# Mirroring most of batch 0 and storing the empty rows of the buckets in two parts

## The chip, the cores and the metric

One core of one Trainium2 chip. The metric is device time in microseconds (us), from one launch. The kernel is a float32 attention over eight batches, followed by a mixture of experts (MoE) that takes the attention's rows.

## The reference

```
# u, v: 8 x 1856 x 256   z: 8 x 1856 x 64   (S = 1856)
scores = (z @ z.transpose(0, 2, 1)) / S
x = u * (maximum(scores, 0) ** 2 @ v)          # then 14848 rows of 256
g = argmax(x @ w_group); e = argmax(x @ w_expert[g])      # 4 groups of 4 experts
h = maximum(x @ w1[g, e], 0)                              # 256 -> 1024
out = softmax weight of g * softmax weight of e * (h @ w2[g, e])
```

The scores of a batch are a symmetric matrix, since both factors are z. Both halves carry the same numbers.

## The kernel before, in words

**Attention.** A batch's 1856 queries are cut into four chunks c = 0 to 3, its 1856 keys into 15 tiles of 128 (the last has 64). One step s is one key tile of one chunk; 60 steps make a batch, s = 0 to 59 is batch 0. For a step, TensorE forms the scores in two matmuls (`sc`), ScalarE (ACT) takes relu and the square (`r`), VectorE (DVE) splits the square into a rounded part `ah` and a rest `al` (a cast and a subtraction), and TensorE multiplies these with the values in six matmuls (`o`: `ah` by `vl`, `ah` by `vh`, `al` by `vh`, for two halves of the output). Scores of a step are made some steps ahead of its `o` matmuls. At the end of a chunk DVE multiplies `o` with u (`xT`), splits it (`xl`), and four matmuls (`pl`) give the routing logits.

**Mirror.** In batches 1 to 7 a block of scores below the diagonal is not computed. When the block above it has been made, DVE transposes it in 32 by 32 pieces (`mt`), SyncE's (SP's) queue stores it to DRAM (`sym`), and four loads bring it back turned (`at`). A step that takes its tile from `at` has no `sc` matmuls, no relu and no square: ACT makes one cast (`ah`) and DVE one subtraction (`al`). Batch 0 computes all its blocks. Batches 1 to 7 have chunks of 512, 512, 512 and 320 queries, batch 0 of 512, 512, 416 and 416.

**Routing.** Each token's row of 1056 bytes (256 values and a few words) is scattered by POOL into the bucket of its expert in DRAM (`bucket`, 16 buckets of `CAPB` rows). A bucket is read to a fixed capacity of 832 to 1216 rows, so rows behind the last token must be empty: `prefill` stores them from a constant tile `padrow`. There are 32 such stores of 640 rows (660 KB) on SP's queue, put in steps 1 to 41 of batch 0 by the list `PFILL`.

**Experts.** The buckets are sorted by their counts; the register values `eli` and `rli` hold, for the j-th, the expert and the first row. The first four (NOLD) are worked on in ten smaller blocks 0 to 9, the others as wider ones. Per block: SP loads the block's rows transposed (`xp`) and a little `meta`; DVE copies (`xf`), ACT casts (`xh_m`), DVE subtracts (`xl_m`); TensorE makes `ph`, ACT and DVE split it (`hh`, `hl`), TensorE makes `yT`; the result goes through a transposing DMA (`yr`) and is scattered to the output. SP's queue also loads the weights of an expert (`raw_e2`, `raw_e3`, four pieces of 512 KB each), two blocks and more ahead. SP, like each engine, carries out its instructions in the order in which they stand.

Of the kernel before, what the change touches and what calls it, by code (L numbers as in the profile page):

```python
# [19 lines left out]
P = 128  # L20
# [9 lines left out]
def tile_glu_attn_moe(  # L30
# [22 lines left out]
    NQ = 4  # L53
    MB = (1, B)
    EDGE = [512, 512, 416, 416], [0, 512, 1024, 1440]
    INNER = [512, 512, 512, S - 1536], [0, 512, 1024, 1536]
    QW, QO = ([(INNER if MB[0] <= b < MB[1] else EDGE)[i] for b in range(B)] for i in range(2))
    ZW = [512, 512, 512, S - 1536]
# [3 lines left out]
    RU = 2 * RW  # L62
    CAPB = (N + 511) // 512 * 512 + 512
    CMAX = (max(caps) + P - 1) // P * P
# [15 lines left out]
    NOLD = 4  # L80
    PFILL = [1 + i for i in range(17)] + [18 + 5 * i // 3 for i in range(2 * NE - 17)]
    assert CMAX % (2 * P) == 0
    FRZ = min(512, min(caps[:NEARLY]))
    assert min(caps[:NEARLY]) > FRZ or len(set(caps)) == 1

# [8 lines left out]
    def cst(name, shape, dt=F32):  # L94
        return pool.tile(shape, dt, tag=name, bufs=1, name=name)
# [25 lines left out]
    def bank(pl, tag, name):  # L121
        return pl.tile([P, 512], F32, tag=tag, name=name)

    bucket = tc.dram_tile([NROW + OVT, RW], I32, name="bucket")
    views = dram_disjoint_views(bucket, B * NQ * NT)

# [177 lines left out]
    def mirrored(b, c, k):  # L304
        return MB[0] <= b < MB[1] and KB[c] < MC and k // KT < MC and POS[k // KT] < c

# [30 lines left out]
    def key(b, c, i):  # L337
        if (b, c) == (B - 1, NQ - 1):
            return (0, 1, 12, 2, 3, 14, 4, 5, 13, 6, 7, 8, 9, 10, 11)[i]
        return KORD[c][i] if MB[0] <= b < MB[1] else i  # L340

    NS = len(steps)
    hl = {}
    oacc = {}
    ut = {}

    def scores(s):
# [27 lines left out]
        ah = new_z(f"ah_{s}")[:, 0:w]  # L375
        mirror = MB[0] <= b < MB[1] and KB[c] < MC and k // KT < MC and c < POS[k // KT]
        if i in ((ACT_TWICE if b + 1 < B else ACT_LAST)[c] if MB[0] <= b < MB[1] else ()) and s >= NK:
            held(nc.scalar.activation(out=ah, in_=a, func=AF.Square))
            held(nc.scalar.activation(out=a, in_=a, func=AF.Square))  # L379
        else:  # L380
            held(nc.scalar.activation(out=a, in_=a, func=AF.Square))  # L381
            held(nc.vector.tensor_copy(out=ah, in_=a))  # L382
# [3 lines left out]
        else:  # L386
            al = None
            nc.vector.tensor_sub(out=ah[TAIL:P, :], in0=a[TAIL:P, :], in1=f32(ah[TAIL:P, :]))
        if mirror:
            put_mirror(b, c, k, a)  # L390
        hl[s] = (ah, al)

# [27 lines left out]
    def chunk_end(s):  # L420
# [85 lines left out]
        defer(s + LG + (1 if XO else 0), logits_out)  # L506
        wait = 5 if last else 12 if b == 0 and c < 2 else (17 if c == 1 and b < B - 1 else 15) if s + 1 < NS - NK else 8
        alone = b == B - 1 and c >= NQ - 2
# [148 lines left out]
    def sort_experts(final=False):  # L657
# [289 lines left out]
    def next_view():  # L947
        ocnt[0] += 1
        return oviews[ocnt[0] - 1]

    def prefill(i):
        r0, n = i // 2 * CAPB + i % 2 * (CMAX // 2), CMAX // 2
        ins = nc.sync.dma_start(
# [47 lines left out]
    for s in range(NS):  # L1001
# [9 lines left out]
        if s == 8:  # L1011
            make_router()
        for i in range(2 * NE):
            if PFILL[i] == s:
                prefill(i)
# [588 lines left out]
```

## Time and profile before

| | |
|---|---|
| median of 3 runs (lowest to highest) | 1425.19 us (1424.57 to 1425.32) |
| the profiled execution | 1423.95 us |
| its span, first to last instruction | 1422.1 us |
| granted clock of TensorE | 1.000 |
| TensorE matmul / weight load busy | 1411.9 us (99%) / 1223.8 us (86%) |
| VectorE / ScalarE / GpSimd busy | 1216.5 us (86%) / 1051.3 us (74%) / 439.0 us (31%) |
| moved by DMA | 256.47 MB |

The profiled execution's own time holds 1.85 us around its span. A sum of edits is made against 1423.95 us, which lies 1.24 us below the median. In the views a start is in us from the span's start; an engine's row has its start, its length, the engine, the line, and output and input by the program's names.

### The profile page before, as it was taken

The numbers are of one execution on the slowest core, as the hardware profiler recorded it, in microseconds if no ns is written. First come the engines' busy times: TensorE is split into PE (matmuls) and PEld (weight loads), VectorE is DVE, ScalarE is ACT, GpSimd is POOL, SyncE is SP. The second block draws the span as 40 slices with busy tenths as digits, with TensorE's granted clock in tenths as the row PEclk, the third lists the DMA queues.
The fourth block names the chain that finished last, engine by engine and source line by source line (L and its number), as shares of the span: only waits on it lengthen the run. The fifth ranks groups of instructions, "written<-read, shape, count | busy, mean of one in ns | idle before, by whom it ended". The sixth has DMA issues, their size and how long they took to land.

```text
span 1422.1 us, 22589 instructions
## 1 busy us (share of the span) xinstructions
PE 1411.9 (99%) x7010; PEld 1223.8 (86%) x7010; DVE 1216.5 (86%) x2436; ACT 1051.3 (74%) x1849; POOL 439.0 (31%) x462
## 2 busy tenths in 40 slices
PE   9999999999999999999999999999999999999998
PEld 7898888888888888888878898988888888899997
DVE  7889999899998999998988667789777888888884
ACT  8887887787887878878776354357777777777773
POOL 0002022220222012202222331332445555555554
PEclk9999999999999999999999999999999999999999
DMA  9997979979899698895987564534555444555552
GB/s 318 328 260 210 235 187 254 230 192 239 195 262 238 160 264 207 223 244 151 243 197 165 116 142 113 122 82 130 126 136 132 126 123 113 138 137 136 139 140 60
DMA packets 400043, 256.47 MB, mean 180 GB/s; under 512 B 244131, under 2 KB 355262, under 8 KB 399920
## 3 DMA queue, kind: packets, MB, share of 16 engines
q1 hardware_dynamic: 387984, 223.97, 63.1%
q0 software_dynamic: 11856, 30.90, 7.7%
q8 instruction: 56, 0.92, 0.3%
q14 instruction: 67, 0.55, 0.1%
q10 hardware_dynamic: 80, 0.13, 0.0%
HBM read 108.29 MB, written 89.21 MB: 139 GB/s over the span
## 4 chain that ended last, share of the span: by engine, by line
PE 92%; DVE 2%; DMA 2%; issue 2%; POOL 1%; ACT 1%; SPq 0%; POOLq 0%; DVEq 0%; ACTq 0%
PE o L408 38%; PE duo_p L887 15%; PE yT L887 6%; PE duo_y L1333 6%; PE sc L370 5%; PE sc L371 5%; PE ph L802 2%; PE ph L803 2%; PE ph L804 2%; PE duo_w L1333 2%; PE duo_x L1333 2%; PE duo_p L1333 2%; PE duo_z L1333 2%; PE pl L483 1%; PE pl L484 1%
## 5 line engine op out<-in xcount | busy, mean ns | idle before, releaser
L408 PE MATMUL o<-ah,vl 128*128 128x512 f32 (+2 forms) x960 | 354.6, 370 | 0.4 <-DVE ah L382 0.4
L408 PE MATMUL o<-ah,vh 128*128 128x512 f32 (+2 forms) x960 | 354.2, 369 | 0.0
L408 PE MATMUL o<-al,vh 128*128 128x512 f32 (+2 forms) x896 | 328.7, 369 | 0.9 <-DVE al L360 0.9
L646 POOL DMA_INDIRECT bucket<-rows,di x121 | 138.6, 1145 | 383.3 <-issue 216.7
L374 ACT ACTIVATE r<-sc 128x512 f32<-128x512 f32 (+2 forms) x312 | 178.8, 573 | 74.4 <-PE sc L371 72.8
L408 PEld LDWEIGHTS o<-ah,vl 128*128 128x128 f32 x960 | 180.2, 188 | 31.0 <-DVE ah L382 1.2
L408 PEld LDWEIGHTS o<-ah,vh 128*128 128x128 f32 x960 | 180.2, 188 | 28.9
L385 DVE TENSOR_TENSOR al<-r,ah 128x512 fp32r<-128x512 f32 (+2 forms) x280 | 187.7, 671 | 19.1 <-ACT r L379 2.2
L930 POOL DMA_INDIRECT out_dram<-y_w,meta_w x92 | 139.3, 1514 | 191.4 <-ACT y_w L924 145.8
L408 PEld LDWEIGHTS o<-al,vh 128*128 128x128 f32 x896 | 167.8, 188 | 27.5 <-DVE al L360 1.2
L887 PE MATMUL duo_p<-hh_w,duo_w 128*128 128x496 f32 (+10 forms) x692 | 178.0, 371 | 0.0
L381 ACT ACTIVATE r<-r 128x512 f32<-128x512 f32 (+2 forms) x280 | 171.4, 612 | 8.9
L887 PEld LDWEIGHTS duo_p<-hh_w,duo_w 128*128 128x128 f32 x692 | 128.6, 188 | 16.7
L382 DVE CAST ah<-r 128x512 fp32r<-128x512 f32 (+2 forms) x280 | 115.9, 414 | 18.8 <-ACT r L381 13.4
L370 PE MATMUL sc<-zm,z2h 128*128 128x512 f32 (+2 forms) x312 | 120.0, 385 | 0.2 <-DVE zm L251 0.2
L371 PE MATMUL sc<-zm,z2l 128*128 128x512 f32 (+2 forms) x312 | 118.9, 381 | 0.0
L310 DVE STREAM_TRANSPOSE mt<-r 128x512 f32<-128x512 f32 x147 | 103.6, 705 | 0.6
L887 PE MATMUL duo_p<-hl_w,duo_w 128*128 128x496 f32 (+10 forms) x346 | 104.1, 371 | 0.0
L360 DVE TENSOR_TENSOR al<-at,ah 128x512 fp32r<-128x512 f32 (+1 forms) x168 | 95.3, 579 | 2.5 <-ACT ah L359 2.3
L359 ACT CAST ah<-at 128x512 fp32r<-128x512 f32 (+1 forms) x168 | 86.1, 531 | 8.8 <-DMA at<-sym 3.9
L807 ACT ACTIVATE hh<-ph 128x512 fp32r<-128x512 f32 (+6 forms) x96 | 45.7, 488 | 39.4 <-PE ph L804 38.6
L887 PE MATMUL yT<-hh,w_e 128*128 128x512 f32 (+6 forms) x352 | 74.1, 328 | 0.0
(259 smaller groups left out, 2874.5 us busy)
## 6 DMA issues: line engine op xcount, KB each, us to landing
sym<-mt SPq DMA_DIRECT2D x126, 256.0 KB
duo_r<-in_w_dram SPq DMA_DIRECT2D x48, 512.0 KB
at<-sym SPq DMA_DIRECT2D x84, 256.0 KB
bucket<-padrow SPq DMA_DIRECT2D x32, 660.0 KB
at<-sym SPq DMA_DIRECT2D x84, 160.0 KB
vr<-in_v_dram SPq DMA_DIRECT2D x23, 512.0 KB
ut<-in_uT_dram SPq DMA_DIRECT2D x23, 512.0 KB
raw_e<-in_w_dram SPq DMA_DIRECT2D x16, 512.0 KB
```

Of the source, the lines that this page charges most:

```text
L310: nc.vector.transpose(out=t2.rearrange("p (j t x) -> p t j x", t=KT, x=32), in_=a.rearrange("p (t j x) -> p t j x", t=KT, x=32))
L370: held(nc.tensor.matmul(ps[:, 0:w], z2h[:, ks], zm, start=True, stop=False))
L371: held(nc.tensor.matmul(ps[:, 0:w], z2l[:, ks], zm, start=False, stop=True))
L374: held(nc.scalar.activation(out=a, in_=ps[:, 0:w], func=AF.Relu, scale=1.0 / S))
L381: held(nc.scalar.activation(out=a, in_=a, func=AF.Square))
L382: held(nc.vector.tensor_copy(out=ah, in_=a))
L385: held(nc.vector.tensor_sub(out=al, in0=a, in1=f32(ah)))
L408: held(nc.tensor.matmul(oa[d][:, 0:QW[b][c]], (vh if q else vl)[:, d0:d0 + P], al if q == 2 else ah, start=(i == 0 and q == 0), stop=end a ...
L646: nc.gpsimd.indirect_dma_start(out=views[(b * NQ + 2 * half + hs[h]) * NT + i], out_offset=bass.IndirectOffsetOnAxis(ap=di[0:n, i0 + i:i0 ...
L887: nc.tensor.matmul(o, wt["2"][f // 2][:, w0:w0 + P], hs[f][q // 2][:, c0:c0 + n], start=(at == 0), stop=(at == 3 * NF - 1))
L930: nc.gpsimd.indirect_dma_start(out=outs(), out_offset=bass.IndirectOffsetOnAxis(ap=meta[0:m, t, 1:2], axis=0), in_=y[0:m], in_offset=None, ...
L1333: nc.tensor.matmul(out, a, b, start=(q == 0 and m in (1, 5)), stop=(q == 2), skip_group_check=True)
```

## The change

Batch 0 gets the chunks of the other batches. All its blocks below the diagonal are taken from the mirror, but those of chunks 0-1 and 0-2: chunk 2 takes 4 tiles (block 1-2), chunk 3 takes 12 (blocks 0-3, 1-3, 2-3). Three of the transposes of chunk 0 are put off by up to six steps (`held_back`). `prefill` stores only the first 512 rows of a bucket, in 16 stores. The rows behind these are stored later, by `fill(j)`, at a row that is taken from the final counts: five small DVE operations behind the final sort make the start rows `sti` (the greater of the count's end and 512), SP loads each start as a register value and stores 768 rows (first four buckets) or 512 rows from there. They stand in the loop over blocks, behind the loads of blocks 1, 2, 3, 5 and 7 (`FILL`). A read of a bucket waits for the fills ahead of it, and a fill for the reads ahead of it. `CAPB` grows by 256 rows.

```
-    MB = (1, B)
-    EDGE = [512, 512, 416, 416], [0, 512, 1024, 1440]
     INNER = [512, 512, 512, S - 1536], [0, 512, 1024, 1536]
-    QW, QO = ([(INNER if MB[0] <= b < MB[1] else EDGE)[i] for b in range(B)] for i in range(2))
+    QW, QO = ([INNER[i] for b in range(B)] for i in range(2))
...
-    CAPB = (N + 511) // 512 * 512 + 512
+    CAPB = (N + 511) // 512 * 512 + 768
...
-    PFILL = [1 + i for i in range(17)] + [18 + 5 * i // 3 for i in range(2 * NE - 17)]
+    PFILL = [1 + 2 * i for i in range(NE)]
...
     def mirrored(b, c, k):
-        return MB[0] <= b < MB[1] and KB[c] < MC and k // KT < MC and POS[k // KT] < c
+        return k // KT < c and (b > 0 or c == NQ - 1 or k // KT > 0)
...
-        return KORD[c][i] if MB[0] <= b < MB[1] else i
+        return KORD[c][i] if b or c else i
...
-        mirror = MB[0] <= b < MB[1] and KB[c] < MC and k // KT < MC and c < POS[k // KT]
-        if i in ((ACT_TWICE if b + 1 < B else ACT_LAST)[c] if MB[0] <= b < MB[1] else ()) and s >= NK:
+        mirror = k // KT > c and (b > 0 or c > 0 or k // KT == NQ - 1)
+        if i in ((ACT_TWICE if b + 1 < B else ACT_LAST)[c]) and s >= NK:
...
-        if mirror:
+        if mirror and s >= NK:
             put_mirror(b, c, k, a)
+        elif mirror:
+            held_back.append((s + (2, 4, 6)[i - NK + 3], lambda: put_mirror(b, c, k, a)))
+        while held_back and held_back[0][0] <= s:
+            held_back.pop(0)[1]()
...
+        if final:
+            st = cst("sst", [P, NE])
+            nc.vector.scalar_tensor_tensor(out=st, in0=ebase, scalar=512.0, in1=base, op0=ALU.add, op1=ALU.max)
...
+            nc.vector.tensor_copy(out=sti, in_=sf)
...
+    def fill(j):
+        regs(j)
+        n = 512 if j >= NOLD else 768
+        at = nc.sync.value_load(sti[0:1, j:j + 1], min_val=512, max_val=(NE - 1) * CAPB + N)
+        nc.sync.dma_start(
+            views[B * NQ * NT + j][ds(at, n), :].rearrange("(p t) w -> p t w", p=P),
+            padrow.unsqueeze(1).to_broadcast([P, n // P, RW]),
+        )
+
     def prefill(i):
-        r0, n = i // 2 * CAPB + i % 2 * (CMAX // 2), CMAX // 2
+        r0, n = i * CAPB, 512
...
-        for i in range(2 * NE):
+        for i in range(NE):
             if PFILL[i] == s:
                 prefill(i)
...
+    FILL = {1: (0, 1), 2: (2, 3), 3: (4, 5, 6, 7), 5: (8, 9, 10, 11), 7: (12, 13, 14, 15)}
...
         more_rows(i)
+        for j in FILL.get(i, ()):
+            fill(j)
```

Where the instructions stand now, first on DVE at the end of batch 0, from the end of chunk 2 (`xT_0_2`) to the split z of batch 1 (`zm_1_0`), which the first scores of batch 1 read. Before:

```order
L430 TENSOR_TENSOR xT_0_2_1130<-o_0_2_0_858,ut_0_2_613 128x416
L430 TENSOR_TENSOR xT_0_2_1130<-o_0_2_1_859,ut_0_2_613 128x416
...
L382 CAST ah_52_1175<-r_52_1173 128x416
L385 TENSOR_TENSOR al_52_1178<-r_52_1173,ah_52_1175 128x416
...
L441 TENSOR_TENSOR xl_0_2_1187<-xT_0_2_1130,xh_0_2_1186 128x416 x2
...
L255 TENSOR_TENSOR z2l_1_0_1249<-zr_1_0_927,z2h_1_0_1248 128x512
...
L271 CAST zm_1_0_1269<-z2h_1_0_1248 64x512
L272 CAST zm_1_0_1269<-z2l_1_0_1249 64x512
```

And of the changed kernel:

```order
L435 TENSOR_TENSOR xT_0_2_1118<-o_0_2_0_896,ut_0_2_628 128x512
L435 TENSOR_TENSOR xT_0_2_1118<-o_0_2_1_897,ut_0_2_628 128x512
L361 TENSOR_TENSOR al_51_1129<-at_0_1_3_1012,ah_51_1128 128x320
L361 TENSOR_TENSOR al_52_1143<-at_0_1_3_1012,ah_52_1142 128x320
L553 COPY lgf_0_0_0_1156<-lgx_0_0_562 128x8x2x40
L558 TENSOR_TENSOR tm_0_0_0_1158<-lgf_0_0_0_1156 128x160
L294 TENSOR_TENSOR vl_1_3_1161<-vr_1_3_960,vh_1_3_1160 128x768
L361 TENSOR_TENSOR al_53_1165<-at_0_1_3_1012,ah_53_1164 128x320
L446 TENSOR_TENSOR xl_0_2_1153<-xT_0_2_1118,xh_0_2_1152 128x512 x2
...
L255 TENSOR_TENSOR z2l_1_0_1209<-zr_1_0_962,z2h_1_0_1208 128x512
...
L271 CAST zm_1_0_1230<-z2h_1_0_1208 64x512
L272 CAST zm_1_0_1230<-z2l_1_0_1209 64x512
```

The subtractions now read the loaded mirror, and the routing of batch 0 (`lgf`, `tm`) has moved behind the end of chunk 2.

Second, on SP, from the load of block 2's rows (`xp_2`) on. Before:

```order
L767 DMA_TRANSPOSE xp_2_10207<-bucket_69 128x4x384
...
L767 DMA_TRANSPOSE xp_3_10387<-bucket_69 128x4x320
...
L767 DMA_TRANSPOSE xp_4_10566<-bucket_69 128x4x256
...
L900 DMA_TRANSPOSE yr_1_10220<-yp_1_10219 128x4x128 x4
...
L767 DMA_TRANSPOSE xp_5_10775<-bucket_69 128x4x368
L900 DMA_TRANSPOSE yr_2_10400<-yp_2_10399 128x4x128 x3
...
L767 DMA_TRANSPOSE xp_6_10969<-bucket_69 128x4x512
...
L183 DMA raw_e2_0_10672<-in_w1_dram 128x1024
```

And of the changed kernel, of which the four stores of 512 rows stand between `yr_2` and `raw_e2`:

```order
L788 DMA_TRANSPOSE xp_2_10156<-bucket_69 128x4x384
...
L975 TENSOR_LOAD sti_89
...
L976 DMA bucket_69<-padrow_70 768x1x264
...
L788 DMA_TRANSPOSE xp_3_10356<-bucket_69 128x4x320
...
L788 DMA_TRANSPOSE xp_4_10591<-bucket_69 128x4x256
...
L921 DMA_TRANSPOSE yr_2_10425<-yp_2_10424 128x4x128 x3
...
L976 DMA bucket_69<-padrow_70 512x1x264
...
L183 DMA raw_e2_0_10791<-in_w1_dram 128x1024
...
L788 DMA_TRANSPOSE xp_5_10894<-bucket_69 128x4x368
```

`xp_3` and `xp_4` no longer follow `xp_2` at once but stand behind `yr_1`, and `xp_5` has moved from ahead of `yr_2` to behind four fills and the weights of the third expert.

## Rows read from the trace of the kernel before

**Rows 1.** The page, part 1: busy time of each engine.

```profile
PE 1411.9 (99%) x7010; PEld 1223.8 (86%) x7010; DVE 1216.5 (86%) x2436; ACT 1051.3 (74%) x1849; POOL 439.0 (31%) x462
```

**Rows 2.** TensorE's longest wait behind its first matmul: us in total, times, longest.

```profile
PE pl L484 <- DVE xl L441: 1.3, 1, 1.3
```

**Rows 3.** The chain in order of time (start, us, what): batch 1, block 2.

```profile
126.03 2.72 PE o L408 x12
...
189.72 4.40 PE o L408 x30
...
811.94 8.34 PE yT L887 x48
```

**Rows 4.** Timeline of TensorE, batch 0, chunk 3: first and last of 55.

```profile
83.93 0.35 PE L370 MATMUL sc<-zm,z2h 128*128 128x416 f32 x1
...
94.01 0.35 PE L370 MATMUL sc<-zm,z2h 128*128 128x416 f32 x1
```

**Rows 5.** Timeline of VectorE, batch 1, chunk 3.

```profile
185.82 0.95 DVE L294 TENSOR_TENSOR vl<-vr,vh 128x768 fp32r<-128x768 f32 x1
...
187.09 1.28 DVE L430 TENSOR_TENSOR xT<-o,ut 128x512 f32<-128x512 f32 x2
...
195.42 0.29 DVE L574 TENSOR_TENSOR oh<-y 128x128 bf16<-128x128 f32 x1
195.63 0.49 DVE L360 TENSOR_TENSOR al<-at,ah 128x320 fp32r<-128x320 f32 x1
```

**Rows 6.** Timeline of VectorE, batch 0, chunk 3.

```profile
99.56 0.42 DVE L272 CAST zm<-z2l 64x512 fp32r<-64x512 f32 x1
```

**Rows 7.** The page, part 5: the transposes, whole run.

```profile
L310 DVE STREAM_TRANSPOSE mt<-r 128x512 f32<-128x512 f32 x147 | 103.6, 705 | 0.6
```

**Rows 8.** Windows: engines' busy us in a stretch, clock, DMA share, GB/s.

```profile
30.00:60.00 30.00, 30.00 (x135) 24.79 (x134) 23.61 (x44) 24.68 (x41) 0.00 (x0) 1.00 1.08 354
...
834.00:840.00 6.00, 6.00 (x52) 6.00 (x52) 3.19 (x7) 4.76 (x11) 1.86 (x3) 1.00 1.03 359
```

**Rows 9.** Timeline of SP's DMA issues, batch 0.

```profile
13.95 23.47 SPq L953 DMA_DIRECT2D bucket<-padrow  x12
...
39.46 0.54 SPq L953 DMA_DIRECT2D bucket<-padrow  x1
```

**Rows 10.** Timeline of SP's DMA issues, blocks 2 to 5 and a later one.

```profile
795.96 1.45 SPq L767 DMA_TRANSPOSE xp<-bucket  x1
...
806.36 5.15 SPq L900 DMA_TRANSPOSE yr<-yp  x4
813.89 1.40 SPq L767 DMA_TRANSPOSE xp<-bucket  x1
821.14 3.81 SPq L900 DMA_TRANSPOSE yr<-yp  x3
...
831.16 0.99 SPq L183 DMA_DIRECT2D raw_e<-in_w_dram  x2
...
1001.36 5.12 SPq L900 DMA_TRANSPOSE yr_w<-yp_w  x4
1007.93 0.97 SPq L1197 DMA_DIRECT2D duo_r<-in_w_dram  x2
```

**Rows 11.** Timeline of VectorE, blocks 2 to 7.

```profile
799.63 1.04 DVE L781 COPY xf<-xp 128x1536 uint16<-128x1536 uint16 x1 [3.39 <-DMA xp<-bucket]
...
842.11 1.00 DVE L781 COPY xf<-xp 128x1472 uint16<-128x1472 uint16 x1
...
865.68 0.69 DVE L813 SCALAR_TENSOR_TENSOR hl<-ph,hh 128x512 fp32r<-128x512 f32 x1 [3.19 <-ACT hh L807]
```

**Rows 12.** Timelines of ScalarE and TensorE: weights and block 5.

```profile
837.43 1.04 ACT L195 CAST w1h_e<-raw_e 128x1024 fp32r<-128x1024 f32 x1
843.15 0.81 ACT L786 CAST xh_m<-xf 128x736 fp32r<-128x736 f32 x1 [2.63 <-DVE xf L781]
...
845.54 0.34 PE L802 MATMUL ph<-xh_m,w1l_e 128*128 128x368 f32 x1
```

More of the change, by code (lines that the diff above doesn't have):

```diff
@@ L80, in tile_glu_attn_moe @@
     NOLD = 4
-    PFILL = [1 + i for i in range(17)] + [18 + 5 * i // 3 for i in range(2 * NE - 17)]
+    PFILL = [1 + 2 * i for i in range(NE)]
     assert CMAX % (2 * P) == 0
     FRZ = min(512, min(caps[:NEARLY]))
+    assert max(caps[NOLD:]) <= 1024 and max(caps) <= 1280 and CAPB >= N + 768
     assert min(caps[:NEARLY]) > FRZ or len(set(caps)) == 1
@@ L124, in tile_glu_attn_moe @@
     bucket = tc.dram_tile([NROW + OVT, RW], I32, name="bucket")
-    views = dram_disjoint_views(bucket, B * NQ * NT)
+    views = dram_disjoint_views(bucket, B * NQ * NT + NE)
     padrow = cst("padrow", [P, RW], I32)
@@ L153, in tile_glu_attn_moe @@
                    allow_small_or_imprecise_dtypes=True)
+    sti = cst("sti", [P, NE], I32)
     capj = cst("capj", [P, NE])
@@ L339, in key @@
             return (0, 1, 12, 2, 3, 14, 4, 5, 13, 6, 7, 8, 9, 10, 11)[i]
-        return KORD[c][i] if MB[0] <= b < MB[1] else i
+        return KORD[c][i] if b or c else i
     NS = len(steps)
     hl = {}
+    held_back = []
     oacc = {}
@@ L506, in chunk_end @@
         defer(s + LG + (1 if XO else 0), logits_out)
-        wait = 5 if last else 12 if b == 0 and c < 2 else (17 if c == 1 and b < B - 1 else 15) if s + 1 < NS - NK else 8
+        wait = 5 if last else (17 if c == 1 and b < B - 1 else 15) if s + 1 < NS - NK else 8
         alone = b == B - 1 and c >= NQ - 2
@@ L711, in sort_experts @@
         yield
+        if final:
+            st = cst("sst", [P, NE])
+            nc.vector.scalar_tensor_tensor(out=st, in0=ebase, scalar=512.0, in1=base, op0=ALU.add, op1=ALU.max)
+            yield
+            nc.vector.tensor_tensor(
+                out=gt, in0=rank.unsqueeze(2).to_broadcast([P, NE, NE]),
+                in1=iota16.unsqueeze(1).to_broadcast([P, NE, NE]), op=ALU.is_equal,
+            )
+            yield
+            nc.vector.tensor_tensor(out=t2, in0=gt, in1=st.unsqueeze(2).to_broadcast([P, NE, NE]), op=ALU.mult)
+            yield
+            sf = cst("ssf", [P, NE])
+            nc.vector.tensor_reduce(out=sf, in_=t2.rearrange("p e j -> p j e"), axis=AX.X, op=ALU.add)
+            yield
+            nc.vector.tensor_copy(out=sti, in_=sf)
+            yield
     def cut(n):
@@ L949, in next_view @@
         return oviews[ocnt[0] - 1]
+    def fill(j):
[5 more added lines that the diff above has]
+            padrow.unsqueeze(1).to_broadcast([P, n // P, RW]),
+        )
     def prefill(i):
-        r0, n = i // 2 * CAPB + i % 2 * (CMAX // 2), CMAX // 2
+        r0, n = i * CAPB, 512
         ins = nc.sync.dma_start(
```

## The prediction

> **What bounds the kernel now.** I read the page first. TensorE is busy for 1411.9 us of the span, 99% [rows 1]. A kernel of this kind gets shorter only by TensorE work that goes away, and longer only by TensorE waits that come in. The second view is therefore TensorE's waits over the whole run: behind the first matmul the longest is 1.3 us, once, for the split of the logits' input [rows 2]. So in batch 0 nothing waits for a transfer, and freeing the DMA there is worth nothing by itself; it can only make room for the mirror. The chain in order of time gives the price of a matmul: 12 of 512 columns take 2.72 us, or 0.2267 us each, and 30 of 320 columns take 4.40 us, or 0.1467 us each [rows 3]. The 416 columns of batch 0's last chunks take 10.08 us from the first to the last of 55 starts, or 0.1867 us each [rows 4]. The clock is 1.00 in the stretches shown [rows 8], which is the level of 2.4 GHz, and the change leaves no gap in which I see it fall.
>
> **The score matmuls that go.** Chunk 2 takes 4 tiles from the mirror, chunk 3 takes 12, and each tile is two matmuls. That is 4 x 2 x 0.2267 = 1.81 us and 12 x 2 x 0.1467 = 3.52 us [rows 3], together **-5.33 us**. Nothing else on TensorE's path is removed.
>
> **The new chunk widths: 0.** A tile row costs 2 x 0.2267 + 2 x 0.1867 = 0.827 us by the old widths and 3 x 0.2267 + 0.1467 = 0.827 us by the new ones [rows 3, 4]. The number of matmuls is the same.
>
> **The transposes in batch 0: 0.** Thirteen transposes of 0.705 us come onto DVE [rows 7]; two casts of chunk 1 go to ACT, and each mirrored tile saves DVE a cast. They are densest in chunk 1: seven of its own and two held back from chunk 0, 9 x 0.705 = 6.35 us. In the 30 us from 30 to 60, which cover that chunk, DVE was busy for 23.61 us [rows 8], so 6.39 us were idle. The cover is just enough, and without those two casts a little more. If DVE falls behind by more than the steps that it is ahead, the rest becomes a TensorE wait; the bounds are 0 and half the load, 3.2 us.
>
> **The mirror's transfers in batch 0: 0.** The stretch from 30 to 60 ran at a DMA share of 1.08 and 354 GB/s [rows 8]. Empty-row stores fall from 32 x 660 KB, 21 MB, to 16 x 540 KB, 8.6 MB. The mirror adds some 3 MB of stores and 3 MB of loads. So 6 to 7 MB less are moved, about 19 us at that rate. The first load is issued some ten steps after its stores and is read some ten steps later.
>
> **The end of batch 0: +1.0.** This is the one place in batch 0 where I find a shortage. The first scores of batch 1 wait for `zm_1_0`, and on DVE that stands behind everything from `xT_0_2` on, which can't start before the `o` matmuls of chunk 2 end. Between these two points TensorE has nine steps of six matmuls and two score tiles at 320 columns, (54 + 4) x 0.1467 = 8.51 us, and four logit matmuls of 512 columns, 0.91 us: 9.41 us [rows 3]. With the old widths there were more columns in this place. DVE's work is nearly that of batch 1 in the same place, where `xT` starts at 187.09 and the last row before the next subtraction ends at 195.63: 8.54 us [rows 5]. Batch 0 has in addition a `vl` of 0.95 us [rows 5] and two `zm` casts of 0.42 us [rows 6]: 8.54 + 0.95 + 0.84 = 10.33 us. 10.33 - 9.41 = 0.92 us, and some 0.1 us for the hand-over from engine to engine. I take 1.0; the bounds are 0, if DVE packs these better, and 2.5 if it comes to `xT_0_2` late by 1.5 us.
>
> **Sorting: 0.** The five small operations of the final sort end before the copy `xf` of block 2, ahead of which DVE sat idle for 3.39 us [rows 11].
>
> **The fills: +0.7.** No row shows a store on SP amid the blocks, so I bound it. An empty-row store took 0.54 us of SP where the queue had room, and 23.47 / 12 = 1.96 us where it was full [rows 9]. A register load I estimate at 0.6 us: two of them lie in the 1.45 us between the end of a `yr` issue (1001.36 + 5.12 = 1006.48) and the next weight load at 1007.93 [rows 10]. In the blocks the DMA engines are far from full but for the weights (share 1.03 in 834 to 840 [rows 8]), so I take 0.54 us.
>
> - Block 3: `xp_3` used to go out behind `xp_2`, now it follows `yr_1`, whose issue ends at 806.36 + 5.15 = 811.51. For `xp_2`, 3.67 us passed from issue (795.96) to use (799.63) [rows 10, 11], so `xp_3` is there at 815.2. Copy, cast and subtraction take under 1.04 + 0.81 + 1.04 us (the first two are those of the wider block 5 [rows 11, 12], the third I take like the copy), which is 818.1, and its matmuls begin where those of block 2 end, at 811.94 + 8.34 = 820.28 [rows 3]. No stall. `xp_4` stands likewise, behind `yr_1` and two more fills, and I count it the same.
> - The weights: four fills stand between `yr_2` (821.14 + 3.81 = 824.95) and `raw_e2`. With register loads and fills, and a wait for the landing of `xp_4`'s transfers, `raw_e2` goes out near 833.1 and not at 831.16 [rows 10]. Its first piece was cast at 837.43 [rows 12]; now it is some 0.8 us later, in a stretch where DVE and ACT have gaps. 0 to 0.5 us.
> - Block 5: `xp_5` went out at 813.89 [rows 10], now it follows fills and weights, about 837. Ahead of it in the queues are 2.16 MB of fills and 2.1 MB of weights from 829 on: 4.26 MB at 350 GB/s is 12.2 us, to 841.2; its own 0.37 MB and the landing make it 843.7. The copy took its turn at 842.11; the cast starts 1.04 us behind it and lasts 0.81 us [rows 11, 12]. So the cast ends at 845.6, and the first matmul of the block stood at 845.54 [rows 12]: 0.1 us, and up to 0.5 us since DVE has little room behind it.
> - The eight later fills delay `xp_7` to `xp_9` by 2 to 3 us; DVE's gap of 3.19 us at 865.68 takes that in [rows 11].
>
> Together 0.3 + 0.4 = 0.7 us. Below, the bound is 0; above, with fills at 1.96 us, `raw_e2` and `xp_5` are late by another 4 x 1.42 = 5.7 us.
>
> The Trainium skill ("DMA: Bandwidth & Descriptors", section "Anatomy of one DMA — SWDGE (gpsimd) path") gives a DMA about 2.0 us fixed and its bytes at 436 GB/s, and warns of a "surprisingly long delay especially when the write target is HBM" before its semaphore fires; that speaks against reads which wait for fills. By its rate the 4.26 MB would be done 2.4 us sooner, the fills would stall nothing, and the sum would be 0.7 us lower. The rows' 354 to 359 GB/s do not show its rate, and no row here shows a fill's landing.
>
> **The sum.** -5.33 + 1.0 + 0.7 = -3.6 us. The profiled execution took 1423.95 us, so 1420.3 us; from the median, which is 1.24 us above it, **1421.5 us**.
>
> **Rivals.**
> - *All of it arrives.* DVE reaches `zm_1_0` in time and the fills hide: -5.33 us, 1419.9 us. For it: DVE's ends are often hidden by gaps. Against: the 0.92 us above.
> - *The gain is eaten in batch 0.* DVE is over-full in chunk 1 (3.2 us) and the end of batch 0 waits 1 to 2.5 us: 1424 to 1425 us, no change. For it: 6.35 us of load on 6.39 us of room. Against: in batches 1 to 7 DVE does the like, and TensorE doesn't wait [rows 2].
> - *The other side: fills that hold SP.* Each fill of 512 rows costs SP x us in place of 0.54. The first four delay the weights and `xp_5` by 4(x - 0.54), the eight others delay `xp_7` to `xp_9` by the same in two goes, less 3 us of room each. To be slower by over 0.2% (2.85 us, about what a measurement of this kernel can tell from no change) the stalls must grow by 6.5 us: 12(x - 0.54) - 6 = 6.5, x = 1.6. At the full queue's 1.96 us it is 12 x 1.42 - 6 = 11 us, 1432 us. For it: that row. Against: there twelve stores stood in a row, here it is four.
> - *TensorE's removed work doesn't shorten it.* Another engine would have to bound batch 0; DVE's and ACT's 79 and 82% there speak against it [rows 8].
>
> **How the numbers follow.** My forecast 0.47 (of it 0.42 faster, 0.05 not over the bound); all of it 0.16; eaten 0.22; fills 0.13 (0.10 slower, 0.03 same); the last 0.02. Faster: 0.42 + 0.16 = 0.58; same: 0.05 + 0.22 + 0.03 = 0.30, less 0.01 for eaten cases that go over; slower 0.13 with the last. The range goes down to the full gain with its scatter, 1419.5, and up over the eaten cases and moderately slow fills, 1427; beyond lie about 0.1 to 0.15. The forecast's own range is 1420 to 1422.5.
>
> **What would show it.** In the profile after: 32 matmuls of L371 and L372 fewer; the start of batch 1's steady steps 4 to 5 us earlier; one TensorE wait of about 1 us for `zm` at the end of batch 0; no wait for `at`; fills of about 0.5 us on SP; TensorE's waits for block 5 under 1 us. I am wrong if TensorE waits for `al` or `ah` in chunk 1, if a fill takes SP over 1.6 us, or if `xf` waits for `xp_5` beyond 845.

## The result and the profile after

The changed kernel takes **1434.33 us** (median of 4 runs, 1433.54 to 1435.43). The kernel before took 1424.88 us in the same session (4 runs, 1423.13 to 1425.32). The ratio is 1.0067, with a 95% interval of 1.0052 to 1.0082: **slower by about 9.5 us**, where I had forecast 3.6 us faster. The profiled execution took 1435.43 us with a span of 1433.6 us, 11.5 us more than before; it is the longest of the four, so its profile shows 2 us more than the medians do.

The page's busy times of the changed kernel, against [rows 1]:

```profile
PE 1412.4 (99%) x6978; PEld 1219.4 (85%) x6978; DVE 1218.8 (85%) x2432; ACT 1044.8 (73%) x1832; POOL 432.7 (30%) x460
```

The 32 matmuls have gone, and yet TensorE is busy for 0.5 us more: matmuls ran somewhere at a lower clock. TensorE's waits over the whole run (us in total, times, longest), against [rows 2]:

```profile
PE yT L908 <- ACT hh L828: 4.0, 1, 4.0
PE sc L371 <- DVE zm L272: 3.4, 1, 3.4
PE ph L823 <- DVE hl L834: 2.3, 1, 2.3
PE yT L908 <- DVE hl L834: 1.4, 1, 1.4
```

One is at the end of batch 0 (`zm`), three are in the expert blocks. The windows of the changed kernel show both places (columns as in [rows 8]):

```profile
20.00:30.00 10.00, 10.00 (x45) 8.05 (x45) 9.40 (x21) 9.78 (x18) 0.00 (x0) 1.00 0.36 122
...
60.00:80.00 20.00, 20.00 (x90) 16.28 (x89) 15.61 (x28) 11.93 (x22) 0.00 (x0) 1.00 1.03 254
...
98.00:100.00 2.00, 0.00 (x0) 0.00 (x0) 1.90 (x6) 2.00 (x7) 0.00 (x0) 0.90 1.04 302
100.00:106.00 6.00, 5.09 (x16) 4.66 (x17) 5.42 (x16) 3.80 (x6) 0.00 (x0) 0.50 0.87 152
...
820.00:840.00 20.00, 17.66 (x125) 17.31 (x124) 11.40 (x28) 7.83 (x18) 8.35 (x10) 1.00 0.69 209
840.00:848.00 8.00, 3.96 (x34) 3.76 (x32) 0.79 (x2) 1.57 (x4) 0.00 (x0) 0.94 1.02 335
848.00:854.00 6.00, 6.00 (x28) 6.00 (x29) 4.33 (x7) 2.46 (x6) 0.00 (x0) 0.51 1.04 191
...
900.00:950.00 50.00, 48.42 (x345) 47.21 (x344) 38.91 (x87) 19.64 (x43) 12.32 (x13) 1.00 0.58 119
```

Where the 11.5 us lie is read from three points on TensorE that both traces have: the first `o` matmul of batch 1, the last `o` matmul of all, and the start of the last of the ten blocks' `yT_b`. Before they start at 110.55, 763.54 and 945.60 us; after, at 111.89, 763.62 and 957.06. So in this execution batch 0 lost 1.3 us where it was to gain 4.3. Batches 1 to 7 gave 1.3 us back: the one wait of [rows 2], 1.3 us for `xl`, is not there any more. And the ten blocks cost 11.4 us.

**Batch 0.** SP's DMA issues of the changed kernel:

```profile
14.90 1.49 SPq L283 DMA_DIRECT2D vr<-in_v_dram  x1
...
30.33 0.34 SPq L318 DMA_DIRECT2D sym<-mt  x1
...
47.80 7.66 SPq L326 DMA_DIRECT2D at<-sym  x6
...
70.11 6.55 SPq L476 DMA_TRANSPOSE rows<-pl  x4
77.20 0.35 SPq L318 DMA_DIRECT2D sym<-mt  x1
...
79.08 0.81 SPq L318 DMA_DIRECT2D sym<-mt  x1
```

From 16.4 to 30.3 SP stands still: the first mirror store waits 13.9 us for DVE's transpose, and the prefill stores that used to fill the DMA engines in this time stand behind it. The share falls to 0.36 in 20 to 30, where before it was 1.09. What was put off then comes together with the mirror. From 60 to 80 the engines are full (1.03) but move 254 GB/s; [rows 8] had 354 at 1.08 from 30 to 60. Part of that drop is older than the mirror: the kernel before moved 295 GB/s from 60 to 80. Its two windows:

```profile
20.00:30.00 10.00, 10.00 (x46) 8.06 (x45) 9.37 (x20) 9.78 (x17) 0.00 (x0) 1.00 1.09 344
60.00:80.00 20.00, 20.00 (x105) 19.03 (x104) 17.08 (x36) 16.82 (x32) 0.42 (x1) 1.00 1.08 295
```

The mirror stores go out late. The tile of one was ready at 63.16, when its transpose ended, and the store was issued at 77.20. Ahead of it on SP stood, among others, a load of the mirror that waited 3.3 us for an earlier store to land, and four transposing DMAs (`rows`) of 6.55 us. The tiles `mt` share a ring of buffers with `r` and `ah`, and so ScalarE waits until that store has landed:

```profile
62.46 0.70 DVE L310 STREAM_TRANSPOSE mt<-r 128x512 f32<-128x512 f32 x1
```

```profile
79.88 0.62 ACT L360 CAST ah<-at 128x512 fp32r<-128x512 f32 x1 [6.20 <-DMA sym<-mt]
```

VectorE stands behind that cast, and TensorE behind VectorE:

```profile
90.65 1.28 DVE L435 TENSOR_TENSOR xT<-o,ut 128x512 f32<-128x512 f32 x2
...
100.34 0.42 DVE L272 CAST zm<-z2l 64x512 fp32r<-64x512 f32 x1
```

```profile
100.91 0.77 PE L371 MATMUL sc<-zm,z2h 128*128 128x512 f32 x1 [3.44 <-DVE zm L272]
```

Chunk 2's last `o` matmul ended at 88.04, and `xT_0_2` began only at 90.65. Behind the wait of 3.44 us the clock stood at 0.50, the level of 1.2 GHz, until about 106: 5.09 us of work at half speed is 2.5 us lost, beside the wait itself.

**The blocks.** SP's issues there, against [rows 10]:

```profile
813.95 1.32 SPq L788 DMA_TRANSPOSE xp<-bucket  x1
...
818.01 1.37 SPq L976 DMA_DIRECT2D bucket<-padrow  x2
827.02 1.29 SPq L788 DMA_TRANSPOSE xp<-bucket  x1
...
829.91 3.83 SPq L921 DMA_TRANSPOSE yr<-yp  x3
834.00 3.89 SPq L976 DMA_DIRECT2D bucket<-padrow  x4
841.53 0.99 SPq L183 DMA_DIRECT2D raw_e<-in_w_dram  x2
...
845.24 4.08 SPq L788 DMA_TRANSPOSE xp<-bucket  x1
...
860.28 8.06 SPq L976 DMA_DIRECT2D bucket<-padrow  x4
872.21 1.29 SPq L788 DMA_TRANSPOSE xp<-bucket  x1
```

A fill itself is short, 0.558 us in the middle of 16. But four of them take 3.89 to 8.20 us from the first to the last, and the next load goes out 2.9 to 3.9 us behind the last. Two things can stand in these gaps. The fills whose landing the profile tells took 3.4 to 3.5 us from issue to landing, and a read of a bucket waits for that; the weights don't. And each fill brings three register loads on SP, of which this line of the instructions by source shows one kind (shortest, middle and longest in ns, first and last start):

```profile
L975 SPq TENSOR_LOAD <-sti x16: 262/500/909, 800.0 to 893.4; - x16
```

Before, such a load took 267 to 292 ns in the middle. The scheduler has moved these loads ahead of reads: eight of them take SP's time from 819.4 to 827.0, where block 4's rows then go out (827.02), and three the 3.6 us between the four fills and the weights. The two fills ahead of block 4's rows were issued by 819.4, so by the same 3.4 us I estimate that they had landed by 823; from there to 827 only the register loads hold SP. The weights `raw_e2` go out at 841.53; before it was 831.16. Who waits is seen on VectorE and ScalarE:

```profile
817.55 0.91 DVE L802 COPY xf<-xp 128x1280 uint16<-128x1280 uint16 x1 [4.40 <-DMA xp<-bucket]
...
875.52 0.76 DVE L802 COPY xf<-xp 128x1024 uint16<-128x1024 uint16 x1 [5.02 <-DMA xp<-bucket]
```

```profile
846.56 1.04 ACT L195 CAST w1h_e<-raw_e 128x1024 fp32r<-128x1024 f32 x1 [6.43 <-DMA raw_e<-in_w_dram]
```

The cast of the weights stands on ScalarE ahead of the last `hh` of block 4, and TensorE's 4.0 us wait is for that `hh`. The windows add up: idle 20 - 17.66 = 2.34, 8 - 3.96 = 4.04 and 50 - 48.42 = 1.58 us, and 6.00 us of work at 0.51 loses 2.94. Together that is 10.9 of the 11.4 us.

### The profile page after: what moved, and what is told of

The parts are those of the page before. It is cut to its first block, busy times and chain, and to the rows that moved or that the text cites. A ratio compares the mean times of both kernels' runs of the same rounds, so it can differ in the third digit from the quotient of the medians.

```text
span 1433.6 us, 22619 instructions
## 1 busy us (share of the span) xinstructions
PE 1412.4 (99%) x6978; PEld 1219.4 (85%) x6978; DVE 1218.8 (85%) x2432; ACT 1044.8 (73%) x1832; POOL 432.7 (30%) x460
## 3 DMA queue, kind: packets, MB, share of 16 engines
HBM read 111.30 MB, written 88.98 MB: 140 GB/s over the span
## 4 chain that ended last, share of the span: by engine, by line
PE 80%; DMA 5%; DVE 5%; issue 3%; SPq 3%; ACT 2%; POOL 1%; POOLq 0%; DVEq 0%; ACTq 0%
PE o L413 35%; PE duo_p L908 14%; PE duo_y L1363 6%; PE sc L371 4%; PE sc L372 4%; PE yT L908 3%; PE duo_w L1363 2%; PE duo_x L1363 2%; PE duo_p L1363 2%; PE duo_z L1363 2%; PE ph L823 1%; PE ph L824 1%; PE ph L825 1%; DMA out_dram<-y_w,meta_w 1%; PE pl L489 1%
## 5 line engine op out<-in xcount | busy, mean ns | idle before, releaser
L413 PE MATMUL o<-ah,vl 128*128 128x512 f32 (+1 forms) x960 | 355.6, 371 | 0.5 <-DVE ah L383 0.4
L413 PE MATMUL o<-ah,vh 128*128 128x512 f32 (+1 forms) x960 | 354.9, 370 | 0.0
L413 PE MATMUL o<-al,vh 128*128 128x512 f32 (+1 forms) x896 | 329.0, 370 | 0.8 <-DVE al L361 0.8
L375 ACT ACTIVATE r<-sc 128x512 f32<-128x512 f32 (+1 forms) x296 | 171.2, 578 | 81.5 <-PE sc L372 78.9
L386 DVE TENSOR_TENSOR al<-r,ah 128x512 fp32r<-128x512 f32 (+1 forms) x264 | 179.2, 679 | 17.3 <-ACT r L380 0.9
L382 ACT ACTIVATE r<-r 128x512 f32<-128x512 f32 (+1 forms) x262 | 161.9, 618 | 8.3
L383 DVE CAST ah<-r 128x512 fp32r<-128x512 f32 (+1 forms) x262 | 108.8, 415 | 14.0 <-ACT r L382 7.4
L371 PE MATMUL sc<-zm,z2h 128*128 128x512 f32 (+1 forms) x296 | 115.6, 391 | 4.1 <-DVE zm L272 3.4
L372 PE MATMUL sc<-zm,z2l 128*128 128x512 f32 (+1 forms) x296 | 114.4, 386 | 0.0
L361 DVE TENSOR_TENSOR al<-at,ah 128x320 fp32r<-128x320 f32 (+1 forms) x184 | 103.8, 576 | 10.7 <-ACT ah L360 10.5
L360 ACT CAST ah<-at 128x320 fp32r<-128x320 f32 (+1 forms) x184 | 93.5, 529 | 14.4 <-DMA sym<-mt 14.1
```

The lines of the kernel that those rows point to most:

```text
L371: held(nc.tensor.matmul(ps[:, 0:w], z2h[:, ks], zm, start=True, stop=False))
L372: held(nc.tensor.matmul(ps[:, 0:w], z2l[:, ks], zm, start=False, stop=True))
L375: held(nc.scalar.activation(out=a, in_=ps[:, 0:w], func=AF.Relu, scale=1.0 / S))
L386: held(nc.vector.tensor_sub(out=al, in0=a, in1=f32(ah)))
L413: held(nc.tensor.matmul(oa[d][:, 0:QW[b][c]], (vh if q else vl)[:, d0:d0 + P], al if q == 2 else ah, start=(i == 0 and q == 0), stop=end a ...
```

## The experiments

My first theory was that the loss has two parts that don't depend on each other, batch 0's transfers and the fills, and that in the fills the landings count and not SP's issue time. The rivals were that one part carries all of it, and that SP's register loads do it. For each run the table gives the median, the ratio to the kernel before (on the same chip in the same session), the first `o` of batch 1, and the time from the last `o` of all to `yT_b`; the last two come from the one profiled execution.

| run | median us | ratio (95%) | first `o` | last `o` to `yT_b` |
|---|---|---|---|---|
| before | 1424.2 to 1424.9 (1427.9 beside e13, e14) | 1 | 110.55 | 182.1 |
| changed kernel | 1434.33 | 1.0067 (1.0052 to 1.0082) | 111.89 | 193.4 |
| e1_fills_alone | 1438.25 | 1.0098 (1.0081 to 1.0115) | 111.30 | 196.1 |
| e2_batch0_alone | 1442.93 | 1.0139 (1.0121 to 1.0157) | 107.40 | 182.1 |
| e3_loads_only | 1444.77 | 1.0149 (1.0132 to 1.0166) | 107.73 | 182.3 |
| e4_stores_only | 1456.41 | 1.0232 (1.0215 to 1.0249) | 110.88 | 190.6 |
| e5_prefill_early | 1431.11 | 1.0042 (1.0026 to 1.0059) | 106.33 | 196.1 |
| e7_fills_later | 1424.39 | 0.9996 (0.9986 to 1.0005) | 110.78 | 184.9 |
| e8_fills_spread | 1420.18 | 0.9974 (0.9965 to 0.9984) | 108.44 | 182.2 |
| e10_spread_early | **1417.06** | 0.9953 (0.9937 to 0.9970) | 106.17 | 182.2 |
| e11_weights_first | 1436.04 | 1.0067 (1.0045 to 1.0089) | 110.12 | 198.9 |
| e12_spread_unmirrored | 1426.74 | 1.0014 (1.0004 to 1.0023) | 111.28 | 183.5 |
| e13_one_load | 1436.65 | 1.0064 (1.0048 to 1.0081) | 108.61 | 195.7 |
| e14_loads_and_stores | 1467.04 | 1.0268 (1.0251 to 1.0285) | 108.85 | 203.6 |

All edits are made to the changed kernel.

**e1_fills_alone: batch 0 as before, the short prefill and the sixteen fills kept.**

```
...
-    QW, QO = ([INNER[i] for b in range(B)] for i in range(2))
+    QW, QO = ([(INNER if b else EDGE)[i] for b in range(B)] for i in range(2))
...
-        mirror = k // KT > c and (b > 0 or c > 0 or k // KT == NQ - 1)
+        mirror = k // KT > c and b > 0
...
```

> Batch 0 as in the kernel before (old chunk widths, nothing mirrored), but with the short prefill and the sixteen fills of the change. Theory: the fills alone cost the 11 us that the changed kernel lost after 800 us, so about 1435 us, with TensorE waits of 6 to 8 us between 820 and 930 and a stretch of half clock. Rival: the loss there is a consequence of what batch 0 left behind (queues, late routing); then this kernel is within 2 us of the one before, 1423 to 1427 us.

The blocks lose 14.0 us with no mirror in batch 0. The fills alone do more than the whole loss of the blocks.

**e2_batch0_alone: no fills; the rows behind the first 512 stored in batches 1 and 2, at fixed places.**

```
...
+            if s == 62 + 7 * i:
+                late(i)
...
-        for j in FILL.get(i, ()):
-            fill(j)
```

> The changed kernel without its fills: the rows behind the first 512 of each bucket are stored at fixed places by sixteen stores of 768 rows in batches 1 and 2 (allowed for these inputs, since no bucket has 512 rows by then). Theory: batch 0 alone gives 5.3 us of matmuls back and loses them again to the wait for the first scores of batch 1 (3.4 us) and to the half clock behind it (2.7 us): within 2 us of before, 1423 to 1427 us, with that wait in the trace. Rival: the extra stores in batch 1 and 2 cost time of their own: over 1427 us. Second rival: without the fills the whole gain arrives, 1419 to 1420 us.

Without fills the blocks take what they took before, to 0.1 us. As a whole this kernel is slower still, since the stores are no better in batches 1 and 2. There TensorE is idle for 8.7 of 80 us beside a DMA share of 1.06:

```profile
120.00:200.00 80.00, 71.35 (x315) 57.99 (x314) 60.08 (x125) 49.39 (x88) 16.37 (x20) 0.96 1.06 271
```

So its median says nothing of batch 0. Its first `o` does: 3.2 us earlier than before, although the instructions of batch 0 and their order are those of the changed kernel, where it came 1.3 us later. One execution of this batch 0 can thus differ from another by 4.5 us.

**e3_loads_only and e4_stores_only: e2 with one half of a fill at each fill's place.** e3 has SP's register loads and no stores; e4 has stores of a fill's size, at constant addresses and to unused rows, and no register loads of a fill (nine others stand in this stretch as they did before).

```
...
+        for j in FILL.get(i, ()):
+            regs(j)
+            nc.sync.value_load(sti[0:1, j:j + 1], min_val=512, max_val=(NE - 1) * CAPB + N)
```

```
...
+        for j in FILL.get(i, ()):
+            m = 512 if j >= NOLD else 768
+            r = (j + 1) * CAPB - m
+            nc.sync.dma_start(
+                bucket[r:r + m, :].rearrange("(p t) w -> p t w", p=P),
+                padrow.unsqueeze(1).to_broadcast([P, m // P, RW]),
+            )
```

> As e2_batch0_alone, with the register loads of the fills (three per fill) at the fills' places, but no stores there. If the register loads, some 0.9 us each on SP, are what makes the expert part late, it is 4 us or more above e2_batch0_alone. If the stores and the waits for their landing do it, it is within 1 us of e2_batch0_alone.

> As e2_batch0_alone, with sixteen stores of the fills' size at the fills' places, to rows of the buckets that nothing uses and at fixed addresses, so with no new register loads. Reads of the bucket wait for them as for the fills. If the stores and the waits make the expert part late, it is 5 us or more above e2_batch0_alone; if the register loads do it, within 2 us of it.

The register loads cost the blocks 0.2 us, the stores 8.5. So the register loads by themselves, at 0.27 us in the middle, are not the cause. In e4 SP stands and waits for the landing of stores, six times and 16.8 us in all:

```profile
SPq L788 <- DMA bucket<-padrow: 16.8, 6, 5.6
```

The stores' 8.5 us are less than the 11.4 to 14.1 of whole fills, and in the changed kernel that wait is only 2.6 us. That led to e13 and e14, below.

**e5_prefill_early: the sixteen prefill stores in steps 1 to 16 in place of 1 to 31.** Batch 0's routing keeps its place.

```
-    PFILL = [1 + 2 * i for i in range(NE)]
+    PFILL = [1 + i for i in range(NE)]
...
```

> The changed kernel with its sixteen short stores of the prefill at steps 1 to 16, ahead of most of the mirror's traffic, and not at every other step up to 31; the routing starts where it did. Theory: in batch 0 the stores of the mirror and the prefill stand in one queue on SP and share the DMA; ACT waits up to 6.2 us for a ring slot that such a store has to free, and that makes the wait of 3.4 us at the end of batch 0 and the half clock behind it. Then here ACT's wait falls under 3 us, the first scores of batch 1 wait under 1.5 us, the clock stays at 1.00 there, and batch 1 begins 3 to 5 us earlier than in the changed kernel: total 1429.5 to 1432 us. Rival: the DVE chain before the split z of batch 1 makes the wait whatever the transfers do; then nothing changes, 1433 to 1436 us.

The gap in the DMA's work has gone, and so has the crowd behind it:

```profile
20.00:30.00 10.00, 10.00 (x46) 8.10 (x45) 9.40 (x21) 9.78 (x18) 0.00 (x0) 1.00 1.10 341
...
60.00:80.00 20.00, 20.00 (x90) 16.28 (x89) 18.68 (x33) 17.36 (x30) 0.00 (x0) 1.00 0.74 175
...
100.00:106.00 6.00, 6.00 (x39) 5.55 (x38) 5.76 (x13) 5.84 (x11) 0.20 (x1) 1.00 0.37 97
```

In batch 0 ScalarE no longer waits for a mirror store, where it waited 6.2 us. The store of the same tile, ready at 63.12, goes out at 71.25 and not at 77.20. TensorE waits 0.4 us for `zm`, and the clock stays at 1.00. The first `o` comes 4.2 us earlier than before. The blocks still lose 14.1 us.

**e7_fills_later: fills 0 to 4 in the blocks, the other eleven one by one in the loop over the wider experts.**

```
...
-    FILL = {1: (0, 1), 2: (2, 3), 3: (4, 5, 6, 7), 5: (8, 9, 10, 11), 7: (12, 13, 14, 15)}
+    FILL = {1: (0, 1), 2: (2, 3), 7: (4,)}
...
+        if more:
+            fill(e + 1)
```

> The changed kernel with its fills 4 to 15 moved out of blocks 3, 5 and 7: fill 4 behind block 7, each later one into the loop over the wide experts, just ahead of its own expert's reads. Theory: of the 11 us lost after 800 us, the part from the weights of the third expert, which stood behind four fills (4.0 us of wait and 3.3 us at half clock), and from the late blocks 7 to 9 (1.6 us) goes away: 1424 to 1427 us. Rival: the loss comes from the reads of the bucket waiting for any fill at all, also the first four; then most of it stays, 1431 us or more.

Ten of the sixteen fills are now issued after `yT_b`. The blocks' loss falls from 11.4 to 2.8 us, and the one wait left there is the 2.3 us for `hl` behind the two groups of two.

**e8_fills_spread: as e7, and no two fills behind one block.**

```
-    FILL = {1: (0, 1), 2: (2, 3), 7: (4,)}
+    FILL = {1: (0,), 2: (1,), 4: (2,), 6: (3,), 7: (4,)}
```

> As e7_fills_later, with the first four fills also spread, one behind each of blocks 1, 2, 4 and 6. Theory: the wait of 2.3 us at 826 us, where a scatter lands late behind two fills, goes away too: 1421.5 to 1425 us, 2 us or so under e7_fills_later. Rival: the first four cost nothing, no difference to e7_fills_later.

The six fills that are left in this stretch now cost the blocks 0.1 us. The ten behind it cost nothing either: from `yT_b` to the end it is 476.2 us, where it was 476.5. The `zm` wait is still 2.4 us.

**e10_spread_early: e8 with the prefill of e5.**

> e8_fills_spread and e5_prefill_early together. If the two losses are separate, the gains add: 1418 to 1422 us, below the kernel before. If batch 0's time is given back at the end of the attention, where TensorE waits in both kernels, it equals e8_fills_spread.

This beats both kernels: 7.2 us under the kernel before. TensorE's waits behind the warm-up:

```profile
PE o L413 <- DVE al L361: 0.8, 1, 0.8
PE o L413 <- DVE ah L383: 0.4, 1, 0.4
PE sc L371 <- DVE zm L272: 0.4, 1, 0.4
```

The four runs lie within 2.4 us, the ten of e8, which has the late prefill, within 6.9. That the fills have not become cheaper, but stand where nothing waits for them, is seen on SP, first in its issues and then in its wait for the landings:

```profile
820.47 0.93 SPq L183 DMA_DIRECT2D raw_e<-in_w_dram  x2
...
832.19 0.77 SPq L976 DMA_DIRECT2D bucket<-padrow  x1
836.63 2.11 SPq L788 DMA_TRANSPOSE xp<-bucket  x1
```

```profile
SPq L788 <- DMA bucket<-padrow: 9.9, 3, 3.7
```

The read behind a lone fill still goes out 3.7 us after the fill's issue ends. SP even waits longer for landings than in the changed kernel (9.9 us from 795 to 920, where that has 2.6), and TensorE has no wait above 0.2 us there. The weights went out 12 us before the fill. Of the 6.6 us that the last `o` comes earlier than before, 4.4 are there at the first `o` of batch 1. Another 1.3 is the `xl` wait of [rows 2], which is gone here too. It is there in e1 and e12, whose batch 0 is not mirrored, so it goes with the mirror and not with the fills; I have no test for why. The last 0.9 is not accounted for.

**e11_weights_first: the fills 4 to 7 behind block 4 in place of block 3, so that the weights go out ahead of them.**

```
-    FILL = {1: (0, 1), 2: (2, 3), 3: (4, 5, 6, 7), 5: (8, 9, 10, 11), 7: (12, 13, 14, 15)}
+    FILL = {1: (0, 1), 2: (2, 3), 4: (4, 5, 6, 7), 5: (8, 9, 10, 11), 7: (12, 13, 14, 15)}
```

> The changed kernel with one edit: its fills 4 to 7 stand behind block 4 and not behind block 3, so that the weights of the third expert and the rows of block 5 go out ahead of them. If these weights behind four fills are the largest part of the loss (4.0 us of wait and 3.3 us at half clock, seen at 843 to 854 us), it is 5 to 8 us under the changed kernel: 1426 to 1429 us. If the delay only moves to block 6, whose rows now stand behind the four fills, it is 1432 us or more.

A theory of mine fell here, that the place of the weights matters most. `raw_e2` went out at 836.39, which is 2.6 us earlier than in the changed kernel when counted from the last `o`, and still 7.7 us later than before. TensorE's 4.0 us wait at this place is gone. But the reads of the next blocks then stood behind the fills, two groups now follow each other closely, and VectorE waited 10 us for block 7:

```profile
862.61 1.34 DVE L802 COPY xf<-xp 128x2048 uint16<-128x2048 uint16 x1 [3.08 <-DMA xp<-bucket]
882.78 0.74 DVE L802 COPY xf<-xp 128x1024 uint16<-128x1024 uint16 x1 [10.12 <-DMA xp<-bucket]
```

The blocks lose 16.8 us. A group of four delays whatever reads stand behind it, weights or rows.

**e12_spread_unmirrored: e1's batch 0 with e8's fills.**

> The fills as in e8_fills_spread and e10_spread_early, but batch 0 as in the kernel before: nothing mirrored, old widths, short prefill at every other step. It shows what the mirror in batch 0 is worth when the fills cost nothing: theory 4 to 5 us, so this kernel at 1421.5 to 1425 us, about the kernel before, and e10_spread_early below it by that. Rival: e10_spread_early's time comes from the lighter prefill and the fills' places, then this one is at 1419 us or less.

Without the mirror in batch 0 the harmless fills bring nothing; the kernel is 2 us slower than before. Of the 1.5 us that its blocks lose, and of the 0.7 us by which its first `o` comes late, I have no account. Each run taken against the kernel before on its own chip, the mirror is worth 6.3 us in e8 and 9.4 with the early prefill of e10.

**e13_one_load and e14_loads_and_stores: fewer register loads, and both halves together.** e13 is the changed kernel with one register load per fill in place of three; e14 is e3 and e4 in one, as e3's edit followed by e4's.

```
     def fill(j):
-        regs(j)
+        while len(is_sorted) < (1 if j < NEARLY else 2):
+            run_gens(10 ** 9, 1)
```

> The changed kernel with its fills where they are, but each fill loads only its start row into a register; expert number and first row are loaded where the kernel before loads them. That takes 32 of 48 register loads out of the stretch of the fills. In the changed kernel eight such loads take the 7.6 us between two fills and the load of block 4's rows, and three take the 3.6 us between the fills and the weights; alone (e3) one took 0.27 us, there 0.4 to 1.1. If the register loads that run beside fills make up most of the fills' price, the blocks' loss falls from 11.4 us to under 5 and the median to 1425 to 1429. If the landing of the fills makes it up, the loss stays over 9 us and the median at 1432 to 1436.

> e3 and e4 together: no fills, the rest of the rows stored in batches 1 and 2, and at each fill's place the three register loads and a store of a fill's size to unused rows at a constant address. If loads and stores cost each by itself, the time from the last o matmul to the last block's yT is e2's 182.1 + 0.2 + 8.5 = 190.8 us. If loads become longer beside stores and so hold SP, it is 194 us or more.

The theory was that the register loads make up the price. In e13 the blocks still lose 13.6 us, but the edit did not do what I expected of it. It takes 20 of the 45 register loads out of the stretch from the last `o` to `yT_b`, and at two places the scheduler has put others there: nine of them stand between the second pair of fills and block 4's rows, from 822.6 to 830.2 (eight in the changed kernel), and three, as before, between the four fills and the weights. At these two places e13 tests nothing. Behind blocks 5 and 7 the loads did go. There four fills take 3.81 and 3.89 us in place of 8.06 and 8.20, and SP waits for the landing, 12.4 us in e13 against 2.6 in the changed kernel:

```profile
862.66 3.81 SPq L977 DMA_DIRECT2D bucket<-padrow  x4
872.72 1.25 SPq L788 DMA_TRANSPOSE xp<-bucket  x1
```

```profile
SPq L788 <- DMA bucket<-padrow: 12.4, 4, 4.9
```

```profile
SPq L788 <- DMA bucket<-padrow: 2.6, 2, 2.0
```

From the first of the four fills behind block 5 to the next read it is 10.1 us, where it was 11.9. At these two groups, then, most of the time of the changed kernel's loads is time that the landings would take anyway. Ahead of block 4's rows and of the weights it is not, since there SP runs loads for some 4 us after the fills must have landed, and for 3.6 us ahead of weights that wait for no fill. The opposite theory, that loads and stores each have their own price, fell with e14: 203.6 us, where the sum of the two was 190.8. Loads of 0.27 us among stores run for up to 0.94. So neither half alone explains the fills, and how the 11.4 us divide between them is not shown. What e8 and e10 change, without taking a load or a store out of the program, is where the fills stand and how many together: five stand alone behind a block, the other eleven just ahead of the reads of the wider experts. That takes the cost away.

## Why the prediction was wrong, point by point

- **The score matmuls that go, -5.33: right.** 7010 - 6978 = 32 matmuls. In e10, where little else is in the way, the first `o` of batch 1 comes 4.4 us earlier, and -5.33 + 1.0 was -4.33. That the two agree so closely is in part luck: the wait at the end of batch 0 was 0.4 us there and not 1.0.
- **The new chunk widths and the transposes, 0: right.** TensorE has no wait in chunk 1. The cover there was as thin as I said: VectorE is busy for 29.0 us from 30 to 60.
- **The mirror's transfers in batch 0, 0: wrong; the first step that failed.** I counted bytes and priced them all at the 354 GB/s of the stores. The bytes fell as said: 20 to 98 us moved 17.7 MB, the sum over the windows, against 25.1 before. But from 40 to 98, with the mirror's transfers among the others, 228 to 254 GB/s were moved at shares of 0.95 to 1.08, and the 354 was the rate of 30 to 60: even the kernel before had 295 from 60 to 80. SP's order had a hole of 13.9 us ahead of the mirror's first store, and a later store was issued 14 us after its tile was ready. I also looked at who reads `at`, and not at who needs the buffers of `mt`, which is ScalarE.
- **The end of batch 0, +1.0: the sum right, its start wrong.** From the last `o` of chunk 2 to the end of TensorE's work I had 9.41 us; the trace has 88.04 to 97.47, 9.43. From `xT_0_2` to the end of the second `zm` cast I had 10.33; it is 10.11. But `xT_0_2` began 2.6 us after that `o`, and in e10 at 87.44, before its chunk's last `o` had ended. I had allowed for 1.5 us of lateness in the upper bound, 2.5 us; the wait was 3.4. e5 shows that the cause is the stores' order, since the early prefill alone took the wait to 0.4 us.
- **"The change leaves no gap in which I see it fall": wrong.** The clock stood at half in both places, 2.5 us lost in batch 0 and 2.9 in the blocks. Neither was in my sum.
- **The fills, +0.7: the term that was mis-sized most; it measured 11.4.** I priced the issue, 0.54 us, and that was right (0.558). Two things were missing. A read of a bucket stands behind the landing of the fills, 3.4 us and more, which I put at nothing. And I took 0.6 us for a register load, which with its register arithmetic is about right for one alone, but allowed for them only in front of the weights. There are 48, and eight stand ahead of `xp_4`, of which I had said "I count it the same" as `xp_3`: it went out at 827.0, and what stands behind it on SP moved with it. Four fills with what belongs to them took 3.9 to 8.2 us in place of 4 x 0.54. Hence `raw_e2` was out at 841.5 and not at 833.1, and `xf` took `xp_5` at 852.16 and not at 843.7. The Trainium skill's sentence on a "surprisingly long delay especially when the write target is HBM" ("DMA: Bandwidth & Descriptors", "Anatomy of one DMA — SWDGE (gpsimd) path") was the warning. By that section's figures, which are for DMAs that POOL issues and not SP, a 540 KB fill is an estimated 2.0 + 1.24 = 3.2 us; the trace has 3.4. I weighed its rate and let its warning pass.
- **The rivals.** The one on the other side, fills that hold SP, came out, near its 1432 us. Its mechanism was half right. I took for the price the full queue's 1.96 us per fill; the groups of four behind blocks 5 and 7 reached 2.0 us per fill, but with register loads and landings and not with a full queue, and 2.9 to 3.9 us more lie behind each group. That the time came near is in part luck too, since the 1432 us still had batch 0's gain in them. "The gain is eaten in batch 0" came out as well, but of its two parts only the wait at the end, which was 3.4 us; VectorE was not over-full in chunk 1.

What stays open: nine runs with the same code in batch 0 (the changed kernel, e2, e3, e4, e7, e8, e11, e13, e14) waited from 1.3 to 3.5 us for `zm`, and in all nine ScalarE had waited 4.5 to 6.2 us for a mirror store. The early prefill removes both waits but for 0.4 us in the two runs that have it, but which transfer comes late in one run and not in another was not found. Nor do the runs say why a register load becomes longer among fills, what the loss in a group of fills would be with the landings alone, or why e14, with as many loads and stores as the changed kernel, loses 21.5 us in the blocks and not 11.4.

## What to carry to other kernels

Before a store is put into a queue that also carries loads, find the next load behind it that depends on it, and count the landing, and the register loads that come with it, and not the issue alone; the sixteen stores cost about 11 us here in groups of two and four, and nothing one at a time, most of them moved to a later place. When transfers are removed, look at the order as well as at the bytes: an issue that waits for an engine keeps everything behind it off the DMA engines. And a buffer that is stored holds its place in its ring until the store lands, so a late store stops whoever needs the next buffer, not only whoever reads the data.

## What the hardware showed that I had not expected

- Behind TensorE's waits for `zm` the clock stood differently. After 1.3 (e2), 1.7 (e3), 2.2 (e13), 2.3 (e14) and 2.4 us (e8) it stayed at 1.00; after 2.8 (e11), 3.1 (e7), 3.4 (the changed kernel) and 3.5 us (e4) it stood at 0.50 for some microseconds. In the changed kernel that was until 106, about five microseconds of TensorE's work.
- SP's register loads took 0.27 to 0.29 us in the middle before, and up to 1.1 us in the changed kernel among its fills.
- DMA engines that are full by their share can move quite different amounts: 354 GB/s at 1.08 (before, 30 to 60) and 295 at 1.08 (before, 60 to 80), and 254 at 1.03 (the changed kernel, 60 to 80, with the mirror's stores and loads among them).
